# Batch 0's first token product by halves of 256 channels, second-product blocks in banks of their own

## The chip, the cores and the metric

The kernel runs on one core of a Trainium2 chip. The metric is the device time of one execution in microseconds; a comparison takes the median of several. The engines are named as in the profile: PE (matmul), PEld (its weight loads), DVE, ACT, POOL, and SP, the engine that issues nearly all DMAs here.

## The reference

Attention over 8 batches, 8 heads, 576 positions and 64 channels a head, then an MLP mixer. Heads 0 to 3 see the last 32 positions (local), heads 4 to 7 see every 32nd position (strided).

```
x   = softmax(mask(q k^T / 8)) v         # x: 576 x 512 per batch, local heads give channels 0-255
h   = relu(x^T w_tok1) w_tok2            # tokens 576 -> 256 -> 576
u   = x + h^T
out = u + relu(u w_ch1) w_ch2            # channels 512 -> 1536 -> 512
```

The four weight matrices come as float64 and are converted on the chip.

## The kernel before

**Products.** Each fp32 factor is split into a high part and the rest (`h` and `l`, type fp32r), and a product is three matmuls: high by high, rest by high, high by rest.

**Names.** `w1` and `w2` are the channel weights `w_ch1` and `w_ch2`, `t1` and `t2` the token weights. `tok1` is the first token product for a batch: it splits x in five chunks of 128 positions (`split`, L555: a high copy on ACT, L559, and a subtraction on DVE, L565), multiplies by t1 (L577), and ends with a relu on ACT and its rest on DVE (L585, L586). `tok2` is the second token product of one block `cc` of 128 channels: it transposes x's block into a PSUM bank (L611), adds six matmuls with t2 (L616), and `split_u` (L594 on ACT, L595 on DVE) splits the sum into `uh` and `ul`. `mlp` runs 12 up-projections (`up_proj`, L815, w1 by columns of 128, relu at L818, rest at L819) and 12 down-projections (`down_proj`, L827, w2), alternating.

**Weights.** `convert` takes one piece of 512 numbers per partition: a DMA (L118), two ACT operations (L128, L131), one DVE operation (L129), and then the join: one DVE operation (L133), an ACT cast to the high part (L142, for the short last piece of t1 L157) and a POOL subtraction for the rest (L143). A generator yields between these three parts. A piece of w1 here is 256 columns of two of the four channel chunks, so up-projections 0 and 1 need two pieces together. There are five pieces of t1 and t2, and 24 of w1 and w2, beside a small tail of t2.

**The opening.** Batch 0's attention, the t1, t2 and first w1 conversions and batch 0's token products stand in one written-out order of generator steps (`steps(...)`, L747 to L769). The order of emission is the order on each engine, SP's queue of DMAs included. `s0`, `s1` are the strided head pairs (`strided_pe`), `l0`, `l1` the local ones (`local_first`); `e` are the weight pieces of the opening, `pieces` those that follow inside batch 0's MLP, two of them begun at each step of `do_pieces`; `mix` is `tok1`, `mixes` (called m0 to m3 in the prediction) are the four `tok2` blocks. The strided result goes to DRAM (L441) and is loaded back (`load_x`, L545, L548); the local result is written into x in SBUF directly (L311), but the last 64 positions go through small DMAs (L309), because `tok1` wants them twice, on partitions 0 to 63 and 64 to 127. `keep_busy` issues idle matmuls (L710).

`tok1` covers all 512 channels in one go. The `tok2` blocks take their PSUM from `Halves`, which deals the two banks of one tile to two blocks:

```
t = pair()
self.left += [t[:, 0], t[:, 1]]
```

The last step of `tok2` for a block issues its six matmuls and its split together:

```
us.append(split_u(pool, pu, apart if turned else []))
yield
```

Batches 1 to 7 do the same products inside the MLP of the batch before (`do_tok1`, `do_tok2`); the strided heads of batches 2 to 7 run on POOL and DVE beside it.

Of the kernel before, what the change touches and what calls it, by code (L numbers as in the profile page):

```python
# [10 lines left out]
F32 = mybir.dt.float32  # L11
# [10 lines left out]
HL = 4  # L22
# [11 lines left out]
WARM = 10  # L34
# [24 lines left out]
def attn_mixer_kernel(ctx, tc, qkT, vw, qkU, vU, qs, ks, vs, qksT, vsP, mask, mask2, w1, w2, wt1, wt2, outT):  # L59
# [111 lines left out]
    def w1_piece(raws, q, c):  # L171

        fs = slice(2 * P * q, 2 * P * q + 2 * P)
        return load_split(raws, lambda: (w1h[:, c:c + 2, fs], w1l[:, c:c + 2, fs]), DM, chunks(w1, c, fs))
# [86 lines left out]
    def local_first(pool, pairs, p, hp, into, masks):  # L261
# [44 lines left out]
        nc.vector.tensor_tensor(out=x_t, in0=av[:, :, n - 1, :D], in1=mz[:, :, n - 1:].to_broadcast([P, 2, D]), op=ALU.mult)  # L306
        x = x_t.rearrange("p j d -> p (j d)")
# [78 lines left out]
    def strided_pe(pool, banks, b, hp, loaded, s_t):  # L386
# [45 lines left out]
        for l in range(2):  # L432
            nc.vector.tensor_tensor(
                out=x_t[:, l::2], in0=sums[l][:, :, :D].rearrange("p (c j) d -> p c j d", j=2),
                in1=mz[:, l].rearrange("p (c j) -> p c j", j=2).unsqueeze(3).to_broadcast([P, NBP // 2, 2, D]), op=ALU.mult)
        x = x_t.rearrange("p m j d -> p m (j d)")
# [105 lines left out]
    def load_x(x_t, b, cs):  # L542
# [4 lines left out]
        for r in range(2):  # L547
            nc.sync.dma_start(out=x_t[64 * r:64 * r + 64, NSC - 1, cs], in_=src[P * (NSC - 1):])  # L548

    def tok1(pool, ps_t, x_t, h, cs, lead=2, room=None):  # L550
# [4 lines left out]
        def split(c):  # L555
            x = x_t[:, c, cs]
            xhl = (room(c) if room else pool.tile([P, 2, DM], F32, name="xhl")).bitcast(F32R)
            xh = xhl[:, 0, :n]
            nc.scalar.copy(out=xh, in_=x)  # L559
            if c == NSC - 1:  # L560
# [3 lines left out]
            xlo = xhl[:, 1, :n]  # L564
            apart.append(nc.vector.tensor_tensor(out=xlo, in0=x, in1=xh.bitcast(F32), op=ALU.subtract))  # L565
            return ((t1h, xh), (t1l, xh), (t1h, xlo))

        ahead = [split(0)]
        yield
        ahead += [split(c) for c in range(1, lead)]  # L570
        ph = [ps_t.tile([P, 512], F32, name="t")[:, :n] for _ in range(2)]
        for c in range(NSC):

            terms = ahead.pop(0)
            for k, (l, r) in enumerate(terms):
                for m in range(2):
                    nc.tensor.matmul(  # L577
                        ph[m], l[:, c, P * m:P * m + P], r, start=(c == 0 and k == 0), stop=(c == NSC - 1 and k == 1))
# [26 lines left out]
    def tok2(pool, ps_t, x_t, h, cc, us, turned):  # L605
# [60 lines left out]
    pieces = [t2_tail, *(lambda raws, c=c: w2_piece(raws, c) for c in range(2))]  # L666
    for k in range(2, 6):
        pieces += [lambda raws, k=k, c=c: w1_piece(raws, k, c) for c in (0, 2)]
        pieces += [lambda raws, c=c: w2_piece(raws, c) for c in (2 * k - 2, 2 * k - 1)]
    pieces += [lambda raws, c=c: w2_piece(raws, c) for c in range(10, NFC)]  # L670
# [14 lines left out]
    with tc.tile_pool(name="first", bufs=2) as first, \  # L685
         tc.tile_pool(name="raws", bufs=4, side="right") as raws, \
# [6 lines left out]
        nc.sync.dma_start(out=mask2_sb, in_=mask2)  # L693
        loaded = [strided_load(first, 0, hp) for hp in range(2)]
        nc.sync.dma_start(out=mask_sb, in_=mask)
# [3 lines left out]
        nc.gpsimd.tensor_copy(  # L699
            out=mask2_b[:, :RP * (NBP - 1)].rearrange("p (c k) -> p c k", k=RP), in_=mask2_sb[:, :RP].unsqueeze(1).to_broadcast([P, NBP - 1, RP]))  # L700
        nc.gpsimd.tensor_copy(out=mask2_b[:, RP * (NBP - 1):], in_=mask2_sb[:, RP:])
        for c in range(NSC):
            nc.gpsimd.tensor_copy(out=masks[:, 64 * c:64 * c + 64], in_=mask_sb[:, FIRST.get(c, 0)])

# [3 lines left out]
        def keep_busy(n):  # L708
            for _ in range(n):
                nc.tensor.matmul(idle_t, still[:, :P], still, start=True, stop=True)  # L710

        class Halves:

            left = []

            def tile(self, shape, dtype, name):
                if not self.left:
                    t = pair()
                    self.left += [t[:, 0], t[:, 1]]
                return self.left.pop(0)  # L720
# [8 lines left out]
        keep_busy(WARM)  # L729
# [3 lines left out]
        s0, s1 = (strided_pe(first, banks, 0, hp, loaded[hp], e_ts[hp]) for hp in range(2))  # L733
        l0, l1 = (local_first(first, ps_p, 0, hp, x_t, masks) for hp in range(2))
        e = [t1_piece(raws, 0), t1_piece(raws, 2), t1_short(raws), t2_piece(raws, 0), t2_piece(raws, 1)]
        e += [w1_piece(raws, q, c) for q in range(2) for c in (0, 2)]

        def room(c):
            return xp.tile([P, 2, DM], F32, name="xhl") if c < 2 else first.tile([P, 2, S], F32, name="eqk") if c < 4 else first.tile([P, 1, 4 * NSC * DV], F32, name="lv")

        mix = tok1(xp, ps_m, x_t, h, slice(0, DM), lead=3, room=room)

        def steps(*gens):
            for g in gens:
                next(g, None)

        steps(l0, l1, l0, l1, *e[:4])  # L747
        steps(s0)
        keep_busy(1)
        steps(s1)  # L750
        keep_busy(1)
# [356 lines left out]
```

## Time and profile before

| | |
|---|---|
| median of 3 runs | 808.65 us (807.28 to 808.75) |
| the profiled execution's own time | 808.64 us |
| its span in the profile | 806.8 us |
| PE busy | 772.2 us (96%) |
| DVE, ACT, POOL busy | 460.5, 240.6, 379.8 us |
| mean granted TensorE clock | 0.989 of full speed |
| chain that ended last | PE 73%, DVE 9%, DMA 5%, POOL 4%, ACT 4%, issue 3% |

A busy share is an average over stages. Times below are us from the span's start unless marked ns. "idle before <-X" names what ended the idle time of an engine; "issue" is idle time for which the profile shows no releaser. [...]

### The profile page before, as it was taken

To read this page: it belongs to the slowest core of one execution; us is meant where nothing else is said; L and a number is where in the kernel's file an instruction comes from. 1 tells how busy PE (TensorE), PEld (TensorE's weight loads), DVE (VectorE), ACT (ScalarE), POOL (GpSimd) and SP (SyncE) were. 2 spreads that over 40 slices of the span, in tenths; PEclk is the share of its full clock that TensorE was granted. 3 is DMA by queue.
4 is the path that set the end of the run, shared out by engine and by line. 5 is a ranking of instruction groups with operands and counts; after the bars stand their busy time and mean duration, and the time that the engine had idled before them with its cause. 6 is when DMAs were issued, how large, how long until landed. Compare 5 with 4: busy or idle time off the path is not lost.

```text
span 806.8 us, 14535 instructions
## 1 busy us (share of the span) xinstructions
PE 772.2 (96%) x5887; PEld 622.0 (77%) x5892; DVE 460.5 (57%) x954; ACT 240.6 (30%) x489; POOL 379.8 (47%) x287
## 2 busy tenths in 40 slices
PE   7659999999999999999999999999999999999998
PEld 4537777777778888888788888788888888888886
DVE  4544666777598677786678667776652234113112
ACT  3556775232122312232223122332123222112110
POOL 1223355959785884678558946776600000202000
PEclk9979999999999999999999999999999999999999
DMA  9456855234822282248305520755042212101001
GB/s 322 143 189 223 252 172 202 82 138 124 246 67 95 67 241 78 70 125 260 122 24 173 174 82 1 226 161 158 1 125 76 82 46 72 53 1 52 1 1 52
DMA packets 70059, 96.40 MB, mean 119 GB/s; under 512 B 33640, under 2 KB 41960, under 8 KB 69992
## 3 DMA queue, kind: packets, MB, share of 16 engines
q1 hardware_dynamic: 69416, 93.57, 37.2%
q10 hardware_dynamic: 576, 1.90, 0.6%
q8 instruction: 46, 0.75, 0.4%
q14 instruction: 21, 0.17, 0.1%
HBM read 67.86 MB, written 27.46 MB: 118 GB/s over the span
## 4 chain that ended last, share of the span: by engine, by line
PE 73%; DVE 9%; DMA 5%; POOL 4%; ACT 4%; issue 3%; SPq 1%; ACTq 0%; DVEq 0%; POOLq 0%
PE acc L827 29%; PE h L815 27%; PE t L616 4%; POOL sprod L452 4%; PE t L577 4%; PE t L815 2%; DMA x<-x 2%; DVE w_f L133 1%; DVE sa L532 1%; PE t L358 1%; ACT w_rest L128 1%; DVE xhl L565 1%; PE t L334 1%; DMA sa<-in_vs 1%; DVE ss L505 1%
## 5 line engine op out<-in xcount | busy, mean ns | idle before, releaser
L452 POOL TENSOR_TENSOR sprod<-sa,ss 128x576 f32<-128x576 f32 (+8 forms) x108 | 153.4, 1466 | 84.7 <-issue 48.7
L452 POOL TENSOR_TENSOR sprod<-sa 128x576 f32<-128x576 f32 (+8 forms) x108 | 160.5, 1518 | 36.9 <-DVE ss L505 11.5
L827 PE MATMUL acc<-gh,w2h 128*128 128x512 f32 x432 | 170.5, 395 | 0.0
L819 DVE SCALAR_TENSOR_TENSOR gl<-h,gh 128x512 fp32r<-128x512 f32 x99 | 68.0, 687 | 179.3 <-ACT gh L818 179.1
L827 PE MATMUL acc<-gh,w2l 128*128 128x512 f32 x432 | 168.4, 390 | 0.0
L827 PE MATMUL acc<-gl,w2h 128*128 128x512 f32 x432 | 168.3, 390 | 0.0
L815 PE MATMUL h<-uh,w1h 128*128 128x512 f32 x396 | 158.5, 400 | 4.1 <-DVE gl L819 2.7
L815 PE MATMUL h<-ul,w1h 128*128 128x512 f32 x396 | 154.9, 391 | 0.0
L815 PE MATMUL h<-uh,w1l 128*128 128x512 f32 x396 | 154.9, 391 | 0.0
L818 ACT ACTIVATE gh<-h 128x512 fp32r<-128x512 f32 x99 | 59.1, 597 | 292.5 <-PE h L815 292.5
L505 DVE TENSOR_REDUCE ss<-sprod 128x9 f32<-128x576 f32 (+8 forms) x108 | 80.4, 777 | 27.8 <-POOL sprod L452 27.6
L827 PEld LDWEIGHTS acc<-gh,w2l 128*128 128x128 f32 x432 | 81.1, 188 | 17.1
L827 PEld LDWEIGHTS acc<-gh,w2h 128*128 128x128 f32 x432 | 81.1, 188 | 17.1
L827 PEld LDWEIGHTS acc<-gl,w2h 128*128 128x128 f32 x432 | 81.2, 188 | 16.5 <-DVE gl L819 0.2
L815 PEld LDWEIGHTS h<-uh,w1h 128*128 128x128 f32 x396 | 74.7, 189 | 23.1 <-DVE gl L819 4.8
L532 DVE TENSOR_REDUCE sa<-sprod 128x64 f32<-128x576 f32 (+8 forms) x108 | 80.2, 776 | 17.5 <-POOL sprod L452 17.1
L815 PEld LDWEIGHTS h<-ul,w1h 128*128 128x128 f32 x396 | 74.7, 189 | 16.1
L815 PEld LDWEIGHTS h<-uh,w1l 128*128 128x128 f32 x396 | 74.8, 189 | 14.7
L644 POOL TENSOR_TENSOR x<-x,xhl 128x512 f32<-128x512 f32 x4 | 5.0, 1280 | 116.1 <-DMA x<-u 116.1
L577 PE MATMUL t<-xhl,t1h 128*128 128x512 f32 x134 | 42.2, 398 | 6.8 <-ACT xhl L559 3.1
L565 DVE TENSOR_TENSOR xhl<-x,xhl 128x512 fp32r<-128x512 f32 x30 | 29.9, 1014 | 11.3 <-ACT xhl L559 11.3
L577 PEld LDWEIGHTS t<-xhl,t1h 128*128 128x128 f32 x134 | 24.3, 188 | 15.3 <-ACT xhl L559 5.3
(177 smaller groups left out, 859.2 us busy)
## 6 DMA issues: line engine op xcount, KB each, us to landing
out_t<-ot SPq DMA_DIRECT2D x35, 256.0 KB
w_raw<-in_w SPq DMA_DIRECT2D x17, 512.0 KB
lqk<-in_qkU SPq DMA_DIRECT2D x9, 832.0 KB
x<-x SPq DMA_DIRECT2D x28, 256.0 KB
lv<-in_vU SPq DMA_DIRECT2D x9, 780.0 KB
xhl<-in_w SPq DMA_DIRECT2D x7, 512.0 KB
x<-lv SPq DMA_DIRECT2D x36, 96.0 KB
xtl<-lv SPq DMA_DIRECT2D x36, 96.0 KB
```

Of the source, the lines that this page charges most:

```text
L128: nc.scalar.activation(out=y_b[:, :, 0], in_=raw_b[:, :n, 3], func=AF.Identity, bias=below, scale=1.0 / 32)
L133: nc.vector.scalar_tensor_tensor(out=a, in0=a, scalar=3, in1=y, op0=ALU.logical_shift_left, op1=ALU.bitwise_xor)
L452: i = nc.gpsimd.tensor_tensor(op=op, **operands)
L505: nc.vector.tensor_reduce(out=s_t[:, i, :i + 1], in_=pr.rearrange("p (n d) -> p n d", d=D), axis=AX.X, op=ALU.add)
L532: nc.vector.tensor_reduce(out=o_t[:, i], in_=pr.rearrange("p (d n) -> p d n", n=i + 1), axis=AX.X, op=ALU.add)
L565: apart.append(nc.vector.tensor_tensor(out=xlo, in0=x, in1=xh.bitcast(F32), op=ALU.subtract))
L577: nc.tensor.matmul(ph[m], l[:, c, P * m:P * m + P], r, start=(c == 0 and k == 0), stop=(c == NSC - 1 and k == 1))
L616: nc.tensor.matmul(pu, l[:, cs], r[:, m, :MAIN], start=(turned and m == 0 and k == 0), stop=(m == 1 and k == 2), skip_group_check=True)
L815: nc.tensor.matmul(ph, l[:, cc, fs], r, start=(cc == 0 and k == 0), stop=(cc == NCC - 1 and k == 2))
L818: nc.scalar.activation(out=gh, in_=ph, func=AF.Relu)
L819: nc.vector.scalar_tensor_tensor(out=gl, in0=ph, scalar=0.0, in1=gh.bitcast(F32), op0=ALU.max, op1=ALU.subtract)
L827: nc.tensor.matmul(acc[cc], l[:, fc, cs], r, start=(fc == 0 and k == 0), stop=(fc == NFC - 1 and k == 2))
```

## The change

- `tok1` for batch 0 runs twice, over 256 channels each: `L` for the local half, `S` for the strided half. All five splits of a half are issued ahead of its matmuls. The last 64 positions are taken once, on partitions 0 to 63, with three terms; the copies to partitions 64 to 127 are gone.
- Each `tok2` block takes a tile of two banks for itself and uses its first bank. Its split is a generator step of its own, after its matmuls.
- A w1 piece is 128 columns of all four channel chunks, the weights of one up-projection. Three are begun in the opening ahead of the last splits, where there were four of the old shape; the `pieces` of the MLP alternate w1 and w2.
- Loads, stores, conversions, attention steps and idle matmuls stand in a new order, one token a generator step; `e0` to `e2` are t1, `e3` and `e4` t2, `e5` to `e7` w1, `p0` to `p3` the first of `pieces`, `x` the reload of the strided half, `b` an idle matmul. 8 idle matmuls at the start, not 10; 6 raw buffers, not 4.

```
-WARM = 10
+WARM = 8
...
+    def w1_piece(raws, fc):
+        fs = slice(P * fc, P * fc + P)
+        return load_split(raws, lambda: (w1h[:, :, fs], w1l[:, :, fs]), DM, w1[:, fs].bitcast(U32).rearrange("(c p) n -> p c n", p=P))
...
-        for r in range(2):
-            nc.sync.dma_start(out=into[64 * r:64 * r + 64, NSC - 1, cs], in_=x[:64])
-        nc.sync.dma_start(out=xd[0][S:S + 64, cs], in_=x[64:])
         nc.vector.tensor_tensor(
             out=into[:, :n - 1, cs].rearrange("p c (j d) -> p j c d", d=D), in0=av[:, :, :n - 1, :D],
             in1=mz[:, :, :n - 1].unsqueeze(3).to_broadcast([P, 2, n - 1, D]), op=ALU.mult)
+        for ps, to in ((slice(0, 64), into[:64, n - 1, cs].rearrange("p (j d) -> p j d", d=D)), (slice(64, P), x_t[64:])):
+            nc.vector.tensor_tensor(out=to, in0=av[ps, :, n - 1, :D], in1=mz[ps, :, n - 1:].to_broadcast([64, 2, D]), op=ALU.mult)
+        yield
+        nc.sync.dma_start(out=xd[0][S:S + 64, cs], in_=x_t[64:].rearrange("p j d -> p (j d)"))
...
+            rows = slice(0, 64 if room and c == NSC - 1 else P)
+            x = x_t[rows, c, cs]
...
-            if c == NSC - 1:
+            if c == NSC - 1 and not room:
...
+            return ((t1h[rows], xh), (t1l[rows], xh), (t1h[rows], xlo))
...
-        ahead = [split(0)]
+        ahead = [split(c) for c in range(1 if lead < NSC else NSC)]
         yield
-        ahead += [split(c) for c in range(1, lead)]
+        ahead += [split(c) for c in range(len(ahead), lead)]
...
             nc.vector.tensor_tensor(out=x_t[:, cc], in0=pu, in1=x_t[:, cc], op=ALU.add)
-            yield
             pu = x_t[:, cc]
-        us.append(split_u(pool, pu, apart if turned else []))
+        yield
+        us[cc] = split_u(pool, pu, apart if turned else [])
         yield
...
-    pieces = [t2_tail, *(lambda raws, c=c: w2_piece(raws, c) for c in range(2))]
...
+    pieces = [lambda raws: w1_piece(raws, 3), lambda raws: w2_piece(raws, 0), t2_tail, lambda raws: w2_piece(raws, 1)]
+    for k in range(4, NFC):
+        pieces += [lambda raws, k=k: w1_piece(raws, k), lambda raws, c=k - 2: w2_piece(raws, c)]
...
+        class Half:
+            def tile(self, shape, dtype, name):
+                return pair()[:, 0]
...
+        gens["L"] = tok1_half(slice(0, HL * D), "eqk", "eqk", "ev", "ev", "es")
+        gens["S"] = tok1_half(slice(HL * D, DM), "xhl", "xhl", "lqk", "lqk", "es")
+        for cc in range(NCC):
+            gens[f"m{cc}"] = tok2(up0, Half(), x_t, h, cc, u, False)
...
+        order = """
+            s0 s1 s1 l0 s0 s0 s1 e0 s0 l0 e0 l0 s0 l1 e1 s1 b e2 l0 e0 e1 l1 l1 b s1 e3 e2 e4 l1 b b e1 s0 s1 e2 e3 e5
+            l0 l1 e4 b b b b m0 L x L L L e3 L e4 L l0 m1 S m3 m0 e6 m0 S e5 S S S e7 e6 S m2 e5 m1 m2 e6 p0 m3 m1 l1 m2 m3 e7 e7
+            p1 p2 p3 p0"""
+        for i, k in enumerate(order.split()):
+            if i == 3:
+                masks_in()
+            next(gens[k], None)
```

## Rows read from the trace of the kernel before

**Rows 1.** Busy time by stage: us, then engines, clock, DMA share, GB/s.
```profile
30.40:60.90 30.50, 19.55 (x73) 13.33 (x73) 14.55 (x29) 17.92 (x32) 8.71 (x8) 0.83 0.53 184
60.90:120.00 59.10, 56.74 (x645) 43.44 (x646) 35.70 (x113) 43.19 (x84) 22.87 (x19) 0.97 0.69 215
120.00:806.00 686.00, 674.99 (x4623) 551.12 (x4621) 395.74 (x786) 168.59 (x358) 343.41 (x243) 1.00 0.34 103
```

**Rows 2.** PE's timeline in the opening: start, us, instructions, idle before.
```profile
15.57 0.81 PE L276 MATMUL pair<-lqk 64*32 64x64 f32 x58 [1.20 <-issue]
...
23.18 1.16 PE L422 MATMUL pair<-ev,es 64*64 64x65 f32 x33 [4.52 <-issue]
...
30.59 1.07 PE L611 MATMUL pair<-ident,x 128*128 128x128 f32 x8 [0.94 <-DVE x L311]
...
39.17 1.07 PE L577 MATMUL t<-eqk,t1h 128*128 128x512 f32 x4
...
44.39 0.39 PE L616 MATMUL pair<-t2h,hl 128*128 128x512 f32 x1
48.90 0.79 PE L616 MATMUL pair<-t2h,hh 128*128 128x512 f32 x1 [4.12 <-DVE ul L595]
...
56.95 0.50 PE L616 MATMUL pair<-t2h,hh 128*128 128x512 f32 x1 [2.67 <-DVE ul L595]
...
60.89 0.79 PE L815 MATMUL h<-uh,w1h 128*128 128x512 f32 x1 [1.40 <-DVE ul L595]
```

**Rows 3.** DVE's timeline: the last write of x's local channels.
```profile
29.77 0.68 DVE L311 TENSOR_TENSOR x<-pair,lm 128x512 f32<-128x512 f32 x1
```

**Rows 4.** DMA queues from 13 to 14.3 us: packets, MB, share.
```profile
q1 hardware_dynamic: 114, 0.51, 97.6%
q8 instruction: 1, 0.02, 5.2%
```

**Rows 5.** DMA queues from 20.3 to 22 us.
```profile
q8 instruction: 1, 0.02, 3.9%
```

**Rows 6.** Busy time by stage: a stretch with a full DMA queue.
```profile
39.00:49.00 10.00, 5.21 (x21) 3.19 (x19) 4.80 (x8) 6.46 (x12) 3.40 (x3) 0.91 1.04 392
```

**Rows 7.** SyncE's queue: x's strided half stored and loaded again.
```profile
19.52 8.65 SPq L441 DMA_DIRECT2D x<-ex  x12
...
29.61 2.05 SPq L545 DMA_DIRECT2D x<-x  x4
```

**Rows 8.** ACT's timeline ahead of the first block's split.
```profile
46.27 0.87 ACT L128 ACTIVATE w_rest<-w_raw,small 128x512 uint8<-128x512 uint8 x1
...
47.55 0.56 ACT L594 CAST uh<-pair 128x512 fp32r<-128x512 f32 x1
```

**Rows 9.** Busy time by stage: the two later stretches at the lower clock.
```profile
47.20:54.10 6.90, 5.20 (x12) 3.80 (x12) 2.31 (x4) 1.80 (x4) 0.52 (x1) 0.51 0.42 162
...
57.40:64.30 6.90, 5.50 (x14) 3.80 (x13) 1.89 (x5) 3.63 (x7) 2.58 (x2) 0.51 0.55 166
```

**Rows 10.** Groups by line, first 61 us: busy us, mean ns, idle before.
```profile
L128 ACT ACTIVATE w_rest<-w_raw,small 128x512 uint8<-128x512 uint8 x8 | 7.0, 875 | 0.6 <-DMA w_raw<-in_wt 0.6
L133 DVE SCALAR_TENSOR_TENSOR w_f<-w_f,w_rest 128x512 uint32<-128x512 uint32 x8 | 5.5, 687 | 0.7 <-ACT w_f L131 0.5
L131 ACT ACTIVATE w_f<-w_raw 128x512 f32<-128x512 f32 x8 | 5.1, 642 | 0.0
...
L595 DVE TENSOR_TENSOR ul<-pair,uh 128x512 fp32r<-128x512 f32 x4 | 2.8, 692 | 10.0 <-ACT uh L594 10.0
...
L143 POOL TENSOR_TENSOR t2l<-w_f,t2h 128x512 fp32r<-128x512 f32 x2 | 2.6, 1288 | 6.3 <-ACT t2h L142 6.3
...
L565 DVE TENSOR_TENSOR xhl<-x,xhl 128x512 fp32r<-128x512 f32 x2 | 1.5, 813 | 2.1 <-ACT xhl L559 2.1
...
L565 DVE TENSOR_TENSOR eqk<-x,eqk 128x512 fp32r<-128x512 f32 x2 | 1.3, 676 | 0.0
...
L157 ACT CAST t1h<-w_f 128x256 fp32r<-128x256 f32 x1 | 0.4, 402 | 0.0
```

More of the change, by code (lines that the diff above doesn't have):

```diff
@@ L384, in strided_load, with strided_pe @@
         return qk_t[:, 0], qk_t[:, 1], v_t
-    def strided_pe(pool, banks, b, hp, loaded, s_t):
+    def strided_pe(pool, banks, b, hp, loaded, s_t, split=False):
         q_t, k_t, v_t = loaded
@@ L545, in load_x @@
             nc.sync.dma_start(out=x_t[:, c, cs], in_=src[P * c:P * c + P])
-        for r in range(2):
+        for r in range(copies):
             nc.sync.dma_start(out=x_t[64 * r:64 * r + 64, NSC - 1, cs], in_=src[P * (NSC - 1):])
@@ L577, in tok1 @@
                     nc.tensor.matmul(
-                        ph[m], l[:, c, P * m:P * m + P], r, start=(c == 0 and k == 0), stop=(c == NSC - 1 and k == 1))
+                        ph[m], l[:, c, P * m:P * m + P], r, start=(c == 0 and k == 0), stop=(c == NSC - 1 and k == len(terms) - 1))
             if c + lead < NSC:
@@ L698, in attn_mixer_kernel, with keep_busy @@
         nc.vector.memset(e_ts[1], 0.0)
[L699 to L703, printed above, removed]
-        idle_t = ps_m.tile([P, 512], F32, name="t")
[L708 to L720, printed above, removed]
+        nc.sync.dma_start(out=mask2_sb, in_=mask2)
+        idle_t = ps_m.tile([P, 512], F32, name="t")
+        def keep_busy():
+            nc.tensor.matmul(idle_t, still[:, :P], still, start=True, stop=True)
         def pair():
@@ L727, in banks @@
             return [t[:, 0], t[:, 1]], [(slice(0, 2), t)]
-        keep_busy(WARM)
+        class Half:
+            def tile(self, shape, dtype, name):
+                return pair()[:, 0]
+        for _ in range(WARM):
+            keep_busy()
         x_t = xp.tile([P, NSC, DM], F32, name="x", bufs=1)
         h = new_h(xp)
-        s0, s1 = (strided_pe(first, banks, 0, hp, loaded[hp], e_ts[hp]) for hp in range(2))
-        l0, l1 = (local_first(first, ps_p, 0, hp, x_t, masks) for hp in range(2))
@@ L735, in attn_mixer_kernel @@
[L735 to L745, printed above, removed]
@@ L766, in attn_mixer_kernel, with strided_first @@
-        steps(e[3], e[7], mixes[0], mixes[1], mix)
-        keep_busy(4)
-        steps(mix, e[3], e[4], e[8], mix, mixes[2], mixes[3], e[4], mix, mix, mix, e[5], e[5], e[6], *pieces[:4])
-        steps(mixes[0], mixes[1], e[6], e[7], mixes[2], e[7], e[8], mixes[3], pieces[0], e[8])
+        u = [None] * NCC
+        def strided_first(hp):
+            qk_t = first.tile([P, 2, S], F32, name="eqk")
+            nc.sync.dma_start(out=qk_t, in_=qksT[0, hp])
+            yield
+            v_t = first.tile([P, NBP // 2, 2, 2, DV], F32, name="ev")
+            nc.sync.dma_start(out=v_t, in_=vsP[0, hp])
+            yield
+            yield from strided_pe(first, banks, 0, hp, (qk_t[:, 0], qk_t[:, 1], v_t), e_ts[hp], split=True)
@@ new lines, in room, with tok1_half, reload, busy @@
+        def room(names):
+            shapes = dict(eqk=[P, 2, S], ev=[P, 2, NSC * DV + DV], es=[P, 2, 32 * NBP * 2], lqk=[P, 2, NSC * P + 32], xhl=[P, 2, DM])
+            return lambda c: (xp if names[c] == "xhl" else first).tile(shapes[names[c]], F32, name=names[c])
+        def tok1_half(cs, *names):
+            return tok1(xp, ps_m, x_t, h, cs, lead=NSC, room=room(names))
+        def reload():
+            load_x(x_t, 0, slice(HL * D, DM), 1)
+            yield
+        def busy():
+            while True:
+                keep_busy()
+                yield
@@ new lines, in attn_mixer_kernel @@
+        gens = dict(x=reload(), b=busy())
+        for hp in range(2):
+            gens[f"s{hp}"] = strided_first(hp)
+            gens[f"l{hp}"] = local_first(first, ps_p, 0, hp, x_t, masks)
+        for i, g in enumerate([t1_piece(raws, 0), t1_piece(raws, 2), t1_short(raws), t2_piece(raws, 0), t2_piece(raws, 1)]):
+            gens[f"e{i}"] = g
+        for fc in range(3):
+            gens[f"e{5 + fc}"] = w1_piece(raws, fc)
+        for i in range(4):
+            gens[f"p{i}"] = pieces[i]
```

53 lines of the change are left out of this document (15 added, 38 removed).

## The prediction, on record before the result

> **What bounds the kernel now.** I read the table by stages first, then PE's timeline in the opening, then what ACT, DVE, POOL and SyncE did in PE's gaps. From 60.9 us on PE is busy 56.7 of 59.1 us, and then 675.0 of 686 [rows 1]: the MLP blocks run on PE almost without a hole, and an edit there must shorten PE's own work. Up to 60.9 nothing is that full: between 30.4 and 60.9 PE is busy 19.6 of 30.5 us, ACT 17.9, DVE 14.6, DMA share 0.53 [rows 1]. That is a chain through several engines, ending when the first w1 product starts at 60.89 [rows 2]. Everything behind hangs on that moment, so the question is when it comes; what it gains the span gains, if the MLP of batch 0 doesn't give it back.
>
> I cut the opening in two at 30.4, when DVE has written the second half of x's local channels [rows 3].
>
> **Up to 30.4: no gain taken.** PE stands still 1.20 us before 15.57 and 4.52 us before 23.18 with no engine or data named ("issue") [rows 2]. Some 1.5 us before PE goes on, at both, a 16 KB packet has passed on the instruction queue [rows 4, 5]; I infer that PE waited for its own program. The second stall, in the second strided product, is what brings x to 30.4. The new order reaches the same product with nearly the same number of instructions before it, so I expect the same stall there, though its first loads are put differently (a t1 piece ahead of the second local pair's keys, both t2 pieces ahead of x's stores). The two missing warm-up matmuls, the earlier start of the strided scores and the earlier l0 transposes all end before that stall and are worth nothing. l1's keys come later by one 0.5 MB piece, about 1.3 us at the 392 GB/s of a full queue [rows 6], and that ends in the stall too. The stores of x's strided half hang on the stalled product as before: issued from 19.52 on, the reload from 29.61 [rows 7]. In front of the reload there is now one w1 piece, again about 1.3 us; x lands near 34, and is wanted near 35. Hidden, with about 1 us of cover; past that, one for one, because the transposes of m3, which stand ahead of m0's product on PE, wait for it.
>
> [...]
>
> **From 30.4 to 60.9: what is removed.** [...]
> - Before, the first token product waits for both halves of x, and its splits stand on ACT behind the t1 and t2 conversions. Now the local half needs no DMA at all.
> - The second-product blocks share a pair of banks, and one block's split is issued together with its products. So m1's first matmul waited 4.12 us and m3's 2.67 us for the split of the block before [rows 2], and that split stood on ACT behind a w1 conversion: the 0.87 us row and its partner run until 47.55, though m0's last product had started at 44.39 [rows 2, 8]. With a bank for each, and the split a step later, m1, m2 and m3 run on: 6.8 us of waits go.
> [...]
>
> **What is added.** 60 matmuls of 256 columns instead of 28 of 512 (three terms for the last 64 rows, no longer two). The trace has no 256-column matmul of this kind. The 512-column ones follow each other every 0.227 us ((1.07 - 0.39)/3, the 0.39 being one matmul's own length) [rows 2]. Bounds: half of that, 0.114, and all of it. I take 0.12, near the lower end, because transposes of 128 columns, which load weights of 128 x 128 each time too, take at most 0.134 (1.07/8, the last one's tail counted in) [rows 2]. [...]
>
> **The new chain, in us of the span,** with durations from [rows 10] and PE at its full clock:
> 1. From 30.2 the five splits of the local half: ACT 0.40 each (the 256-column row), DVE about 0.4, between half and the whole of its 0.68 for 512 columns. PE has its first pair near 30.7, and 30 x 0.12 = 3.6, held up a little by DVE: 34.5.
> 2. Relu and its rest, 0.4 + 0.4 and a hand-over: 35.4. m0's six products wait for t2's second low half. That is the last of a chain behind DVE's splits: two joins of 0.69, a cast, POOL 1.28 twice, to 36.4. m0 ends at 37.1.
> 3. The strided half's splits ran meanwhile; its 30 matmuls: 40.7.
> 4. Its relu and rest lie beside m2's transposes and m1's six products (0.5 + 6 x 0.227 = 1.9): 42.6. m2 and m3, 12 x 0.227 = 2.7: 45.3.
> 5. The last split, ACT 0.56 [rows 8] + DVE 0.69 + 0.2 of hand-over: 46.8.
> 6. Handing over and contention: of two pairs of like subtractions one has a mean of 813 ns and one 676 [rows 10]; I add 0.7 for some ten such steps. The first up-projection starts at **47.5**.
>
> Against 60.9 that is 13.4. PE is dense from 37 to 45, so I take the full clock for the first up-projection: 3.4 us at half speed before [rows 9] are worth 1.7 more.
>
> **What is given back.** Three w1 pieces of 128 columns are begun ahead of the last splits where four pieces were; the third's conversion and half of the fourth's now stand on ACT behind the last split and ahead of the first relu: 2 x (0.88 + 0.64) + 0.6 = 3.6 by their rows [rows 10], with 2.7 us of up-projection over it. The relu is late by about 1, and the same later for DVE and the joins. ACT is busy 43.2 of 59.1 us in that stage [rows 1], so it recovers. Cost: 0 to 3.6; I take 1.0, as PE has two up-projections to go before it needs the first relu. The w1 pieces are as many bytes and conversions as before, with rows of 1 KB where they had 2 KB; DMA has room (0.69 share [rows 1]). Later pieces keep leads of 2.5 to 5 blocks of twelve matmuls. Nothing else in batches 1 to 7 changes its order on any engine: the additional yield in the second product only moves a split's issue, and splits follow one another as before.
>
> Sum: 13.4 + 1.7 - 1.0 = 14.1. The profiled execution took 808.64 us (span 806.8), within 0.01 of the median; 808.64 - 14.1 = **794.5 us**.
>
> **Rivals.**
> - *No stall, or a shorter one:* the second local half then waits for its loads and ACT's conversions, so at most about 4 of the 4.5 us come back: 790.5. For it: the new order changes what DMA carries at that moment. Against: the stall's place in the program stays.
> - *256 columns cost what 512 do:* 60 x (0.227 - 0.12) = 6.4 more: 801. For it: each still loads a full block of weights, and no row shows that 256 columns hide it. Against: the transposes' pace.
> - *Batch 0's MLP gives back some of it:* fewer pieces ahead; if relus and joins stay late by the 3.6 us, and up-projections 2 and 3 wait for w1 in turn, some 6 are lost: 800.5. Against: ACT's 16 us of idle time in that stage.
> - *Slower:* instruction blocks wait behind data. If each further block that PE needs comes only when the data queue is empty, the stall grows, for the opening's loads now follow one another with fewer holes. It decides when PE's stalls together exceed today's 5.7 by more than 14.1 us; waiting for the last opening loads, near 45, would put the up-projection near 63 and the time at 810. Against: the first packet [rows 4] went through while the data queue was at 97.6%.
>
> **Chances.** Forecast 0.62 (own range 791 to 799: the bounds of 256 columns below, of the give-back, and a stretch at 1.2 GHz, worth 1.7 to 3.4); shorter stall 0.10; dear 256 columns 0.10; given back 0.11; slower 0.07. The range 790 to 803 leaves out the slower case and the tails of the first and the third. Measurements of this kernel tell changes of about 0.2% (1.6 us): faster 0.91, within it 0.03, slower 0.06.
>
> **What would show it.** Right: the first w1 product near 47.5 at the full clock, second products of the four blocks with no wait for another block's split, a 256-column matmul every 0.12 us, the 4.5 us issue stall still there. Wrong: a longer or missing stall; a matmul pitch near 0.23; PE gaps before up-projections 2 and 3; m3's transposes waiting for the reload.

## The result, and the profile of the changed kernel

798.26 us (median of four runs, 797.42 to 799.21) against 808.1 us: ratio 0.988, interval 0.9862 to 0.9896, so 9.8 us faster. Forecast were 794.5 us, a gain of 14.1. The profiled execution, the longest of the four (799.21), has a span of 797.4 us, 9.4 less than before, and that is the difference the rows below account for.

Busy time by stage of the kernel after; the columns are those of [rows 1]:

```profile
30.40:44.20 13.80, 13.80 (x92) 12.21 (x91) 9.30 (x21) 9.49 (x20) 4.55 (x4) 1.00 0.87 281
44.20:120.00 75.80, 70.71 (x700) 53.94 (x699) 44.26 (x127) 53.65 (x102) 29.63 (x24) 0.95 0.71 223
120.00:797.50 677.50, 663.85 (x4569) 542.51 (x4568) 391.46 (x778) 162.18 (x347) 338.13 (x239) 1.00 0.32 99
```

The stretch from 30.4 to the first w1 product is 13.8 us long, where [rows 1] show 30.5, and PE fills all of it. But PE is idle for 5.1 us of the next 75.8 and for 13.7 us behind that; before it was 2.4 us in the MLP's first 59 and 11 behind [rows 1].

PE's timeline of the opening after, against [rows 2]:

```profile
20.70 0.69 PE L421 MATMUL pair<-ev,es 64*64 64x65 f32 x29 [1.48 <-issue]
...
29.15 0.50 PE L579 MATMUL t<-eqk,t1h 128*128 128x256 f32 x2 [0.90 <-ACT eqk L561]
...
30.03 0.74 PE L579 MATMUL t<-eqk,t1h 128*128 128x256 f32 x4
...
40.09 0.47 PE L618 MATMUL pair<-t2h,hh 128*128 128x512 f32 x1
...
44.30 0.39 PE L825 MATMUL h<-uh,w1h 128*128 128x512 f32 x1
```

The stall in the second strided product is 1.48 us where it was 4.52. The local half's product runs from 29.15, the blocks m1 to m3 from 40.09 without a wait, and the first up-projection starts at 44.30, with nothing idle before it. The split of the last block, on DVE, ends behind that start, at 45.8:

```profile
45.12 0.69 DVE L597 TENSOR_TENSOR ul<-pair,uh 128x512 fp32r<-128x512 f32 x1 [0.61 <-ACT uh L596]
```

To find where the rest went I laid PE's order of work side by side at the same products. First come four landmarks of the kernel before (a fifth stands in [rows 2]), then those of the kernel after:

```profile
69.90 0.50 PE L815 MATMUL h<-uh,w1h 128*128 128x512 f32 x1
...
80.52 0.50 PE L815 MATMUL h<-uh,w1h 128*128 128x512 f32 x1
...
146.72 0.60 PE L611 MATMUL t<-ident,x 128*128 128x128 f32 x4
...
150.73 0.39 PE L827 MATMUL acc<-gh,w2h 128*128 128x512 f32 x1
```

```profile
51.62 0.50 PE L825 MATMUL h<-uh,w1h 128*128 128x512 f32 x1
...
66.43 0.50 PE L825 MATMUL h<-uh,w1h 128*128 128x512 f32 x1
...
132.76 0.60 PE L613 MATMUL t<-ident,x 128*128 128x128 f32 x4
136.81 0.66 PE L613 MATMUL t<-ident,x 128*128 128x128 f32 x4 [3.45 <-DVE hl L588]
...
141.65 0.40 PE L837 MATMUL acc<-gh,w2h 128*128 128x512 f32 x1
```

| landmark on PE | before | after | lead |
|---|---|---|---|
| first up-projection [rows 2] | 60.89 | 44.30 | 16.6 |
| third up-projection | 69.90 | 51.62 | 18.3 |
| fourth up-projection | 80.52 | 66.43 | 14.1 |
| batch 1's second token product | 146.72 | 132.76 | 14.0 |
| first down product behind it | 150.73 | 141.65 | 9.1 |
| end of the span | 806.8 | 797.4 | 9.4 |

So the opening and the first two up-projections gave 18.3 us, more than forecast, and 4.2 and 4.9 us were given back in two places. From 141.65 to the end the lead changes by 0.3 us only.

**First place, 50 to 62 us.** PE's waits there, and ACT's timeline:

```profile
54.15 0.30 PE L197 MATMUL t<-lqk 64*32 64x64 f32 x2 [0.87 <-DVE gl L829]
55.24 0.45 PE L197 MATMUL t<-lqk 64*32 64x64 f32 x30 [0.80 <-DVE es L401]
...
58.91 0.80 PE L632 MATMUL t<-hh,t2h 128*128 128x512 f32 x1 [0.75 <-POOL t2h L143]
```

```profile
48.96 0.58 ACT L828 ACTIVATE gh<-h 128x512 fp32r<-128x512 f32 x1
...
52.28 0.60 ACT L142 CAST w2h<-w_f 128x512 fp32r<-128x512 f32 x1
52.79 0.58 ACT L828 ACTIVATE gh<-t 128x512 fp32r<-128x512 f32 x1
56.12 0.76 ACT L404 ACTIVATE es<-es 128x648 f32<-128x648 f32 x1 [2.75 <-DVE es L401]
```

The second up-projection's last product ends at 49.9, and its relu comes at 52.79: between the two relus ACT has two conversions and two casts of weight pieces. Its rest on DVE comes late, then DVE's reductions of the strided scores, then the exponential (ACT idle 2.75 us), then t2's tail, and PE waits 0.87, 0.80 and 0.75 us. In the same piece of work the kernel before has one wait of this size:

```profile
77.89 0.44 PE L224 MATMUL t<-ident,ls 128*128 128x128 f32 x2 [1.03 <-ACT es L413]
```

That makes 1.4 us more of waiting. The rest of the 4.2 us, 2.8, is clock (an estimate: the 5.65 us in which PE is busy at 0.51 would be 2.9 at 1.00):

```profile
56.00:62.40 6.40, 5.65 (x17) 4.15 (x16) 2.60 (x14) 4.80 (x12) 0.46 (x1) 0.51 0.66 218
```

After the first two of these gaps PE was granted 0.51 of its clock for 6.4 us; the third gap lies inside that stretch. (A stretch at 0.51 is what the prediction's chances and relu_first's expectation call one at 1.2 GHz; the profiles show the share alone, no frequency.)

**Second place, 130 to 141 us.** ACT's, DVE's and POOL's timelines of the kernel after:

```profile
132.37 0.62 ACT L142 CAST w2h<-w_f 128x512 fp32r<-128x512 f32 x1 [3.10 <-DVE w_f L133]
134.91 0.62 ACT L142 CAST w2h<-w_f 128x512 fp32r<-128x512 f32 x1 [1.92 <-DVE w_f L133]
135.44 1.08 ACT L587 ACTIVATE hh<-t 128x512 fp32r<-128x512 f32 x2
...
130.31 2.03 DVE L133 SCALAR_TENSOR_TENSOR w_f<-w_f,w_rest 128x512 uint32<-128x512 uint32 x1
...
133.59 1.30 DVE L133 SCALAR_TENSOR_TENSOR w_f<-w_f,w_rest 128x512 uint32<-128x512 uint32 x1
136.06 1.29 DVE L588 SCALAR_TENSOR_TENSOR hl<-t,hh 128x512 fp32r<-128x512 f32 x2 [1.18 <-ACT hh L587]
...
128.31 3.48 POOL L453 TENSOR_TENSOR sprod<-sa 128x512 f32<-128x512 f32 x2
```

The relu of batch 1's token product stands on ACT behind the casts of the last two weight pieces, each of which waits for its join on DVE. Before, one such cast stood there, the relu followed at 145.12, and PE waited 0.18 us:

```profile
144.59 0.62 ACT L142 CAST w2h<-w_f 128x512 fp32r<-128x512 f32 x1 [2.67 <-DVE w_f L133]
...
147.50 0.66 PE L611 MATMUL t<-ident,x 128*128 128x128 f32 x4 [0.18 <-DVE hl L586]
```

The changed opening begins one w1 piece fewer, so the list that batch 0's MLP works off has 22 pieces in place of 21, and the 22nd's join falls at step 18.5, ahead of that relu. PE waits 3.45 us, and its 12 second products behind that take 4.4 us where they took 2.8, partly at the lower clock (0.50 from 138.0 to 141.4): 3.3 more of waiting and 1.6 of clock are the 4.9. The two joins took 2.03 and 1.30 us beside POOL's instructions, for 0.69 with none of POOL's beside them [rows 10]; how much of the wait is owed to that, and not to their place, no run takes apart.

### The profile page after: what moved, and what is told of

Read it like the earlier page. It is cut to its first block, busy times and chain, and to the rows that moved or that the text cites. A ratio compares the mean times of both kernels' runs of the same rounds, so it can differ in the third digit from the quotient of the medians.

```text
span 797.4 us, 14592 instructions
## 1 busy us (share of the span) xinstructions
PE 770.7 (97%) x5916; PEld 623.6 (78%) x5916; DVE 463.4 (58%) x963; ACT 241.4 (30%) x496; POOL 379.4 (48%) x287
## 4 chain that ended last, share of the span: by engine, by line
PE 76%; DVE 9%; DMA 5%; POOL 4%; issue 2%; ACT 2%; SPq 1%; DVEq 0%; ACTq 0%; POOLq 0%
PE acc L837 31%; PE h L825 28%; PE t L618 5%; PE t L579 5%; POOL sprod L453 4%; PE t L825 2%; DMA w_raw<-in_wt 2%; DMA sa<-in_qs 1%; PE t L357 1%; DVE sa L533 1%; DVE xhl L567 1%; PE t L632 1%; DVE w_f L133 1%; DVE w_rest L129 1%; DVE ss L506 1%
## 5 line engine op out<-in xcount | busy, mean ns | idle before, releaser
L837 PEld LDWEIGHTS acc<-gh,w2l 128*128 128x128 f32 x432 | 81.2, 188 | 17.2
L533 DVE TENSOR_REDUCE sa<-sprod 128x64 f32<-128x576 f32 (+8 forms) x108 | 80.1, 777 | 17.2 <-POOL sprod L453 16.9
L579 PE MATMUL t<-xhl,t1h 128*128 128x512 f32 (+1 forms) x134 | 41.2, 390 | 5.1 <-DVE xhl L564 2.5
L561 ACT CAST xhl<-x 128x512 fp32r<-128x512 f32 (+1 forms) x37 | 21.9, 609 | 42.7 <-PE t L579 36.4
L567 DVE TENSOR_TENSOR xhl<-x,xhl 128x512 fp32r<-128x512 f32 (+1 forms) x30 | 29.3, 996 | 9.2 <-ACT xhl L561 9.2
```

Of the source, the lines that this page charges most:

```text
L533: nc.vector.tensor_reduce(out=o_t[:, i], in_=pr.rearrange("p (d n) -> p d n", n=i + 1), axis=AX.X, op=ALU.add)
L579: nc.tensor.matmul(ph[m], l[:, c, P * m:P * m + P], r, start=(c == 0 and k == 0), stop=(c == NSC - 1 and k == len(terms) - 1))
L837: nc.tensor.matmul(acc[cc], l[:, fc, cs], r, start=(fc == 0 and k == 0), stop=(fc == NFC - 1 and k == 2))
```

## The experiments

All ratios are to the kernel before, run beside on the same chip; the change itself has 0.9879.

**The two losses.** Two kernels put the last pieces elsewhere, one puts the second relu first, one does two of these.

tail_early:

```
-            at(int(1.8 * i) / 2, do_pieces, i)
+            at(int(1.8 * i) / 2 - (0, 0.5, 0.5, 1)[max(0, i - 18)], do_pieces, i)
```

> The last three weight pieces go half a block, half a block and one block of twelve matmuls earlier (16.5, 17.5, 17.5 in place of 17, 18, 18.5). Theory: the 3.45 us in which TensorE waits for batch 1's second token product, near 133, comes from the casts of the last two pieces, which stand on ScalarE ahead of the token product's relu; moved ahead they leave it, the gap falls below 1 us and the stretch at the lower clock behind it goes: 798.3 - 4 = about 794 us. Rival 1: VectorE is full there with its reductions and joins, and what comes earlier is only paid earlier: the gap stays over 2.5 us, time within 1.6 us of 798.3. Rival 2: the gap belongs to the GpSimd products that share time with VectorE, same outcome.

802.04 us, 0.9926 (0.9899 to 0.9953): slower than the change. PE's timeline:

```profile
133.60 1.22 PE L579 MATMUL t<-xhl,t1h 128*128 128x512 f32 x2 [7.20 <-DVE xhl L564]
```

The gap didn't shrink, it moved to the token product itself and doubled. The joins, 3.68 us for two on DVE at 126.96, and their casts on ACT, the second at 130.68, now stand ahead of the split of x's last rows (ACT 131.69, DVE 132.54). The first rival had DVE full, and it is busy 8.79 of 10 us from 120 to 130; but what comes earlier is not only paid earlier, it hurts an earlier consumer, and more.

tail_late:

```
-            at(int(1.8 * i) / 2, do_pieces, i)
+            at({20: 19, 21: 19.5}.get(i, int(1.8 * i) / 2), do_pieces, i)
```

> The last two weight pieces are joined later, at steps 19 and 19.5 in place of 18 and 18.5, so that both stand behind batch 1's token-product relu. Theory of ScalarE's order: the relu no longer waits for two casts, TensorE's 3.45 us gap near 133 falls to under 1 us, 794 us or a little less. Rival: VectorE is the one that is late, whatever order; then the gap only shrinks by the one join taken from in front of it (1.3 us) and the time stays at 796.5 to 798.

796.38 us, 0.9847 (0.9831 to 0.9862). The wait ahead of L613 is gone altogether, and the clock from 130 to 140 is 1.00. In this profile the lead at the first down product behind is 15.9 us, in place of 9.1. Then PE waits anew:

```profile
154.74 1.16 PE L333 MATMUL t<-lqk 64*32 64x64 f32 x94 [1.35 <-DVE x L634]
162.42 0.50 PE L825 MATMUL h<-uh,w1h 128*128 128x512 f32 x1 [0.82 <-DVE gl L829]
```

So the order on ACT and DVE was the cause of the gap, as the theory said, though the time lies nearer to the rival's 796.5 than to its 794: 2.2 us of waiting come back where DVE, behind with its strided sums (busy 9.96 of 10 us from 150 to 160), comes late to the next consumer. The same kernel has the code of the change up to 120 us, with the three waits of the first place (0.87, 0.80 and 1.61 us), but a clock of 1.00 there:

```profile
56.00:62.00 6.00, 4.39 (x21) 3.35 (x22) 3.09 (x15) 5.22 (x13) 0.45 (x1) 1.00 0.88 269
```

Its lead falls by 2.3 us in the first place, not by 4.2: 1.9 us of the change's first loss is a stretch at a granted 0.51 that the same code doesn't always get. (By itself the stretch costs the 2.8 us estimated above, but the third wait is shorter beside it, 0.75 us for 1.61.)

relu_first:

```
-            at(int(1.8 * i) / 2, do_pieces, i)
+            at(1 if i < 2 else int(1.8 * i) / 2, do_pieces, i)
```

> In batch 0's MLP the conversion of the second, third and the join of the first two weight pieces go behind the second relu (steps 1 and 1 in place of 0 and 0.5). Theory: ScalarE's backlog put the second relu 2.9 us behind the end of its products, from which TensorE's gaps near 53 to 59 (0.87, 0.80, 0.75 us) and then the stretch at 1.2 GHz from 56.4 to 62.4 came; with the relu first the gaps and the stretch go, the lead over the kernel before stays near 18 up to the first down-projection, and the time falls by 3.5 to 4.5 us, to 794 or 794.5. Rival: the conversions are needed as early as this; put off by one block, the t2 tail or the first w2 piece comes late and TensorE waits there instead: within 1.6 us of 798.3.

797.14 us, 0.9856 (0.9839 to 0.9873), not to be told from the change by time alone. ACT and PE:

```profile
48.98 0.60 ACT L828 ACTIVATE gh<-t 128x512 fp32r<-128x512 f32 x1 [0.39 <-PE t L825]
...
53.25 0.45 PE L197 MATMUL t<-lqk 64*32 64x64 f32 x30 [0.71 <-DVE es L401]
56.85 0.50 PE L632 MATMUL t<-hh,t2h 128*128 128x512 f32 x1 [1.56 <-POOL t2h L143]
```

The relu now follows its products, the 0.87 wait is gone, 0.80 became 0.71, and the clock stays at 1.00. The tail product's wait stays: t2's tail is converted no earlier. Against the 3.28 us of waits in tail_late's profile 2.27 remain, so the backlog was worth 1.0 us in waits; the theory named the right relu but put too much on it. Its profile has a clock of 0.66 from 130 to 140, the change's 0.90, which takes away some of that win.

both (relu_first and tail_early together):

> Both edits, the relu ahead of the conversions at the start of batch 0's MLP and the last three pieces earlier at its end. If both theories hold the two gains add: 798.3 - 8 = about 790 us. If the second loss only takes up what the first gives back (the pieces all run ahead of a fixed limit of VectorE's), about 794.

799.7 us, 0.9888 (0.9863 to 0.9914). Neither number came. The waits of 0.71 and 1.56 us are those of relu_first, the 7.20 us wait at L579 that of tail_early; the two places don't act on each other.

combined (relu_first, tail_late, and batch 0's tail product from step 2 to 3):

```
-        at(2 if b == 0 else 0, tok2_tail, ps_t, x_t, h, b)
+        at(3 if b == 0 else 0, tok2_tail, ps_t, x_t, h, b)
...
-                at(int(1.8 * i) / 2, do_pieces, i)
+                at({0: 1, 1: 1, 20: 19, 21: 19.5}.get(i, int(1.8 * i) / 2), do_pieces, i)
```

> The second relu of batch 0's MLP ahead of the conversions, the tail product of batch 0 one block later (step 3 in place of 2), and the last two weight pieces behind batch 1's token-product relu. If the losses are independent: relu_first won some 1.1 us in TensorE's waits, the tail product's wait of 1.56 goes as well, and tail_late won 4.9 less the 2.15 that VectorE's strided sums gave back near 153 and 161: 798.3 - 1.1 - 1.5 - 2.7 = 793 us, ratio to the kernel before 0.981. Rival: the strided sums on VectorE are a limit of their own in 115 to 165, and whatever is won ahead of it is waited for near 153: the lead at batch 1's tenth block stays at 13.9 us as in tail_late, 796 us, ratio 0.985.

793.3 us, 0.9819 (0.9801 to 0.9838), a clear gain over the change. In the first place the 0.71 us wait is left, beside a new one of 0.34 at 61.84; the lead at the fourth up-projection is 17.8 us, and at the first down product behind batch 1's token product 18.3. The limit near 150 holds as in tail_late, at the same two places:

```profile
152.28 1.15 PE L333 MATMUL t<-lqk 64*32 64x64 f32 x94 [1.36 <-DVE x L634]
159.96 0.50 PE L825 MATMUL h<-uh,w1h 128*128 128x512 f32 x1 [0.86 <-DVE gl L829]
```

But it takes 2.1 us of the lead and not everything that was won ahead of it: in tail_late the lead there was 15.9 us ahead of the two waits and 13.8 behind them, here 18.3 and 16.3. The rival, a fixed limit, falls.

strided_earlier (combined, and `if b or i >= 14` in place of 16 ahead of some_strided):

> The combined kernel with the strided lane of batch 2 begun two blocks earlier (steps from 14 in place of 16). The combined kernel lost 2.1 us of its lead near 151 and 159, where TensorE waits for VectorE. Theory: the strided sums are late there because they begin late; begun earlier the two waits (1.36 and 0.86) shrink below 0.4 each and the time falls to 791.5 or so, ratio 0.9795. Rival: earlier sums take VectorE from the last weight pieces and the token product's splits, and the waits come back between 108 and 130: 793 us or more.

797.5 us, 0.9853 (0.9826 to 0.988): the rival. The first wait near 150 (now at 162) falls to 0.62 us and the second is gone, but two waits ahead of them grow, from 1.15 to 1.87 us at 110 and from 1.07 to 2.36 at 133, and two are new, 2.52 us at 120 and 2.71 at 140:

```profile
139.87 0.66 PE L613 MATMUL t<-ident,x 128*128 128x128 f32 x4 [2.71 <-DVE hl L588]
```

**The parts of the change.**

shared_banks:

```
-            def tile(self, shape, dtype, name):
-                return pair()[:, 0]
+            def tile(self, shape, dtype, name):
+                if not self.left:
+                    t = pair()
+                    self.left += [t[:, 0], t[:, 1]]
+                return self.left.pop(0)
...
+        half = Half()
...
-            gens[f"m{cc}"] = tok2(up0, Half(), x_t, h, cc, u, False)
+            gens[f"m{cc}"] = tok2(up0, half, x_t, h, cc, u, False)
```

> Only the banks are undone: the second-product blocks share a pair of banks again, two by two, in the new order with the split a step later. If it is the shared bank that made TensorE wait (4.12 and 2.67 us in the kernel before, as the prediction put it), waits of that kind come back ahead of the blocks behind the first, up to 6.8 us, and the time goes to 803 to 805. Rival: the order does it, since now no product has a split of the same pair still open ahead of it: no such wait over 0.3 us, time within 1.6 us of 798.3.

798.07 us, 0.9875 (0.9854 to 0.9897). ACT, then PE:

```profile
44.88 0.59 ACT L596 CAST uh<-pair 128x512 fp32r<-128x512 f32 x1 [1.31 <-PE pair L618]
...
47.68 0.47 PE L831 MATMUL h<-uh,w1h 128*128 128x512 f32 x1 [2.84 <-DVE ul L597]
```

No second product waits: of the 6.8 us none comes back there. Instead the third block's split waits until the products of the fourth, in the same pair, are done, and the up-projection until the last split is done. The banks are thus worth 2.8 us at this place. The time didn't show it: the waits of 0.87 and 0.80 us in the first place are gone, since ACT catches up while PE waits, so 1.5 us are left at the fourth up-projection (lead 14.2, against 15.7 in tail_late), and in the profile its clock was 0.998 on the mean, the change's 0.991.

shared_split_now (the same, and each split right behind its products):

```
- ... m0 e6 m0 S e5 S S S e7 e6 S m2 e5 m1 m2 e6 p0 m3 m1 l1 m2 m3 e7 e7
+ ... m0 m0 e6 S e5 S S S e7 e6 S m2 e5 m1 m1 m2 m2 e6 p0 m3 m3 l1 e7 e7
```

> The banks shared as above, and each block's split issued right behind its products, as in the kernel before. If bank and order act together: m3's first product waits for m2's split, about 1.5 us (ScalarE 0.56, VectorE 0.69, handing over 0.2), the others for nothing since m0's split is done long before; time 799.5 to 800.5. If the banks alone: 6.8 us as above. If neither: within 1.6 us of 798.3, and the waits of the kernel before came from the conversions ahead of the splits alone.

800.16 us, 0.9902 (0.9884 to 0.992), as the first case had it:

```profile
44.11 0.50 PE L618 MATMUL pair<-t2h,hh 128*128 128x512 f32 x1 [1.40 <-DVE ul L597]
47.27 0.47 PE L831 MATMUL h<-uh,w1h 128*128 128x512 f32 x1 [1.49 <-DVE ul L597]
```

A wait of one split, 1.4 us, is what the shared bank cost this product, with nothing else ahead of the split; the second line, 1.49 us, is the up-projection waiting for the last split. By the rows of before, the rest of the 4.12 and 2.67 us [rows 2] was what stood on ACT ahead of the split: m0's last product ended at 44.78 [rows 2], its split began at 47.55 [rows 8], 2.8 us later. The order takes that away; this part is worked out from the rows and not run by itself.

whole (batch 0's first token product in one go of 512 columns, 28 products, ahead of all second products):

```
-        gens["L"] = tok1_half(slice(0, HL * D), "eqk", "eqk", "ev", "ev", "es")
-        gens["S"] = tok1_half(slice(HL * D, DM), "xhl", "xhl", "lqk", "lqk", "es")
+        gens["S"] = tok1_half(slice(0, DM), "xhl", "xhl", "eqk", "eqk", "lv")
...
-            l0 l1 e4 b b b b m0 L x L L L e3 L e4 L l0 m1 S m3 m0 e6 m0 S e5 S S S e7 e6 S m2 e5 m1 m2 e6 p0 m3 m1 l1 m2 m3 e7 e7
+            l0 l1 e4 b b b b m0 x e3 e4 l0 m1 S m3 e6 S e5 S S S S m0 e7 m0 e6 m2 e5 m1 m2 e6 p0 m3 m1 l1 m2 m3 e7 e7
```

> Batch 0's first token product in one go of 512 columns, begun when the strided half of x is back, with everything else of the change left in. By the prediction's terms the local half's 30 products of 256 columns (29.2 to 33.6 in the profile) then lie behind the reload: with the 28 products of 0.227 (6.4 us) in place of 3.9 for the second half, and m0 behind them, the first up-projection comes 2.5 to 4 us later, 47 to 48, time 801 to 802.5. Rival: the halves are hidden anyway, ScalarE's and VectorE's conversions of t2 and w1 set the time of the up-projection: it stays near 44.5, time within 1.6 us of 798.3.

804.06 us, 0.9954 (0.9936 to 0.9972), 5.8 us above the change, more than either number expected.

```profile
31.52 1.59 PE L613 MATMUL pair<-ident,x 128*128 128x128 f32 x4 [2.23 <-DMA x<-x]
...
49.42 0.39 PE L824 MATMUL h<-uh,w1h 128*128 128x512 f32 x1
```

The up-projection comes 5.1 us later. PE waits 2.23 us for the reload and then has the 28 products ahead of it, the first of them at a granted clock of 0.66 on the mean from 30 to 35; later m2's transposes wait 1.40 us for m0's split, which frees their bank. By this run the halves are the larger part of the change, 5.8 of its 9.8 us, with these two counted in: they fill the time of the reload. The parts need not add up.

w1_square (the old cut of the w1 pieces, 256 columns of two row blocks):

```
-        return load_split(raws, lambda: (w1h[:, :, fs], w1l[:, :, fs]), DM, w1[:, fs]. ...)
+        return load_split(raws, lambda: (w1h[:, c:c + 2, fs], w1l[:, c:c + 2, fs]), DM, chunks(w1, c, fs))
```

> Only the cut of the w1 pieces is undone: 256 columns of two row blocks each as in the kernel before, so that an up-projection needs two pieces where it needed one; the same number of pieces, begun in the same places. Theory: the cut by 128 columns is worth nothing here. GpSimd has the first two pieces' low halves at 43.4 and 44.7, the first up-projection's second half wants the second one at 45.7 and nothing waits; the first up-projection comes near 44.5 and the time is within 1.6 us of 798.3 (ratio 0.986 to 0.990). Rival: it is what lets the products begin; then TensorE waits for GpSimd's low halves inside the first or third up-projection, 1 to 3 us, ratio 0.990 to 0.992.

797.21 us, 0.9849 (0.9822 to 0.9877): the cut is worth nothing here. The wait at batch 1's second product is there as in the change, 3.46 us, and the list still has 22 pieces. PE's timeline, then the stage from 130 to 140:

```profile
135.29 0.66 PE L613 MATMUL t<-ident,x 128*128 128x128 f32 x4 [3.46 <-DVE hl L588]
...
130.00:140.00 10.00, 6.54 (x34) 5.31 (x33) 7.92 (x12) 3.89 (x7) 8.72 (x8) 1.00 0.42 133
```

But the clock stays at 1.00 here, and the 12 second products behind the wait take 2.8 us, as in the kernel before. Like the 1.9 us in the first place, the 1.6 us of clock in the second don't come with every such wait: this profile has the change's waits in both places at full clock, and gives back 5.9 us (a lead of 18.2 at the third up-projection, 12.3 at the end) where the change's gives back 8.9.

**The stall named "issue".** In the profiles of the eleven kernels that have the change's order up to there it stands ahead of the same product, 29 from the end of L421's second run, and is between 0.59 and 3.33 us; the two 16 KB packets of the instruction queue ahead of it (46 packets, 0.75 MB in the whole execution, before and after; that they carry PE's program is inferred from the stalls) pass 6.9 to 7.6 us apart (10.70 and 18.07 in the change, 13.01 and 20.59 before), and the third follows 3.8 to 6.0 us behind. Two kernels alter what the data queue carries, and leave PE's order; light_queue also puts the t1 conversions later.

light_queue:

```
- ... s0 l1 e1 s1 b e2 l0 e0 e1 l1 l1 b s1 e3 e2 e4 l1 b b e1 s0 s1 e2 e3 e5
+ ... s0 l1 s1 b l0 e0 l1 l1 b s1 l1 b b s0 e1 e2 e3 e4 s1 e1 e2 e1 e2 e3 e5
```

> The loads of four weight pieces (two t1, two t2, 1.6 MB) go behind the first strided stores, so that the data queue runs empty near 15 in place of 24. In the traces so far the second 16 KB instruction packet comes 7.0 to 7.6 us after the first and TensorE stands still before the 29th-last product of L421 for 0.6 to 4.5 us. Theory A: the packet waits behind the data; then it comes 2 to 5 us after the first, and the stall at that product is gone (under 0.3 us). Theory B: TensorE's program has a pace of its own, some 7.3 us for 16 KB whatever the queue carries: the packets stay 7.0 to 7.6 us apart and the stall at that product is 1 us or more. The kernel itself should be slower by 2 to 6 us, since the t1 conversions come late.

800.35 us (one run). PE, and the queues from 15.9 to 17.2 us:

```profile
17.92 1.23 PE L421 MATMUL pair<-ev,es 64*64 64x65 f32 x48 [0.25 <-ACT t1h L142]
...
26.21 1.31 PE L298 MATMUL pair<-lv,ls 64*32 64x65 f32 x70 [3.70 <-issue]
```

```profile
q1 hardware_dynamic: 116, 0.29, 56.7%
q8 instruction: 1, 0.02, 4.9%
```

All 48 products run in one go; the packet passed at 16.09, 4.5 us after the first, just as the data queue, full until then (share 1.05 from 14 to 16), had thinned out. The next one, with the moved loads now in the queue, passed 7.2 us later, and the stall appears at the next boundary, 3.70 us.

heavy_queue:

```
- ... l1 l1 b s1 e3 e2 e4 l1 b b e1 s0 s1 e2 e3 e5
+ ... l1 l1 b s1 e3 e2 e4 e5 e6 l1 b b e1 s0 s1 e2 e3
...
- ... m3 m0 e6 m0 S e5 S S S e7 ...
+ ... m3 m0 m0 S e5 S S S e7 ...
```

> Two more pieces (1 MB of w1) are loaded ahead of the strided stores, so that the queue stays full some 2.6 us longer. Theory A: the third instruction packet, 3.8 to 6.0 us after the second so far, comes 6 us or more after it, and TensorE stands still by issue ahead of L298 or the first local products. Theory B: it comes 3.8 to 6 us after it as before. The strided half comes back up to 2.6 us later; the first up-projection moves by 0 to 2 us.

799.17 us (one run). The third packet passed 6.5 us after the second (17.84, 24.36), and PE stood still:

```profile
26.83 0.93 PE L298 MATMUL pair<-lv,ls 64*32 64x65 f32 x70 [2.06 <-issue]
```

Both go with the first theory, light_queue clearly, heavy_queue narrowly: 6.5 us against up to 6.0, and a wait of 2.06 us at a product where the change's own order shows up to 1.51. A fixed pace of some 7.3 us is out. That data in the queue is what holds a packet back is likely and not shown: in light_queue the share of the data queue was 1.02 over the 4.5 us between the first two packets and 0.76 over the 7.2 us behind them, and when PE asks for a packet no profile tells. Why the stall differs between 0.59 and 3.33 us with one and the same order these runs don't settle.

## Why the prediction was right in kind and 4 us off

- **Up to 30.4, "no gain".** Wrong, in two steps: that the same place in the program means the same stall, and that the stall is what brings x. The stall was 1.48 us for 4.52; as the same order has 0.59 to 3.33 in eleven profiles, its size here is in part luck. x's local half was complete at 28.85 (DVE, 28.58 + 0.27) in place of 30.45 [rows 3], but a shorter stall didn't bring it: in those profiles it was complete between 27.90 and 29.69, at 28.61 with the stall of 3.33 (tail_early), at 29.69 with one of 0.75 (both). Other waits take its place, in the change those for l0's and l1's exponentials (1.61 and 1.01 us). Which part of the new order makes x earlier stays open. In light_queue one packet passed without a stall, at 16.09, and all 48 products ran on; elsewhere the stall at this place was 0.59 to 4.52 us.
- **256 columns at 0.12 us.** Right: four in 0.74 us, (0.74 - 0.40) / 3 = 0.113; over the second half, with the steps between its tiles, 30 from 35.84 to 39.68, 0.128.
- **The chain of five steps.** Durations right within 0.6 us. L ended near 33.5, m0 35.8, S 39.7, m1 41.6, m3 44.3; the forecast was 34.5, 37.1, 40.7, 42.6, 45.3, later by 1.0 to 1.3 throughout, where x was forecast 1.6 later than it came. The reload stayed hidden, as forecast: m3's transposes ran at 33.50 with m1's, without a wait.
- **"The last split, 46.8", and 0.7 of handing over: 47.5.** Wrong by 2.2 us. The step put the last split ahead of the up-projection. The up-projection started behind m3's last product; the fourth block is read only by its last three products, from 46.34, when the split was done (45.8). shared_banks shows the forecast's case: with the split on the path PE waits 2.84 us and starts at 47.68.
- **Shared banks, 6.8 us.** The waits went, but the term's owner was wrong: shared_split_now prices the bank alone at one split, 1.4 us a time. The order took the rest.
- **The clock, 1.7.** Right: the lead grew from 16.6 to 18.3 over the first two up-projections. (Before, the last four of m3's products ran at the lower clock too and are not in this term.) That a dense PE is granted the full clock, on which the term rests, no run shows: PE had 1.00 while busy for all of 30.4 to 44.2, but 0.50 while busy for all of 28 to 30 in light_queue.
- **Given back, 1.0.** This is the term that failed: 8.9, or 5.9 where the clock stayed full (w1_square). Half was at the place it named. It reckoned with one late relu and with ACT's idle time over the stage; the first was late by 1.8 (its products ended at 47.2), the second by 2.9, and an average of idle time doesn't help an instruction that stands behind conversions. The other half lies under "nothing else in batches 1 to 7 changes its order": I counted bytes and conversions, which are equal, but not the pieces left for the MLP, 22 for 21, nor where the last one falls.

In sum 16.6 + 1.7 - 8.9 = 9.4, where the forecast had 13.4 + 1.7 - 1.0 = 14.1. Two errors work against each other here, 3.2 us too little for the opening and 7.9 too little given back, and that the time came within 4 us is in part luck. The rival of a shorter stall had its condition come true, but not its 4 us: x came 1.6 earlier, and 1.0 of that was left at the end of m3's products. The rival "batch 0's MLP gives back some of it" was right in kind (800.5), through the late relu it named and, near the end of the same MLP, through a second place that it didn't; the waits for w1 that it expected didn't come. The rival of dear 256 columns fell. That of instruction packets behind data pointed the right way in light_queue and heavy_queue, but its condition, that each packet waits until the queue is empty, doesn't hold: the change's own came at 18.07 while the queue was full (share 1.01 from 17.8 to 19.3). The stall didn't grow, so the slower case didn't come.

Open: why the stretches from 56 to 62 us and behind the wait at 136.81 were granted 0.51 and 0.50 in the change's profile, and 1.00 in others with the same waits (tail_late, w1_square).

## What to carry to other kernels

Work moved out of a tuned opening has to be followed to the step where it now falls: list the deferred items, count them, and see which engine has them ahead of something due. The wait of 4.12 us at a shared bank was, by the rows of before, 2.8 us of what stood ahead of the split on ACT and the split itself; in shared_split_now, with the banks still shared and a new order, only the split's own length was left, 1.4 us. Deferring a piece past the instruction that is due (tail_late) helped, hurrying it (tail_early) hurt an earlier one: beside a DVE busy 8.8 of 10 us, look at who comes next.

## What the runs showed of the hardware

- The instruction queue passed packets of 16 KB, 46 with 0.75 MB in all, before and after. PE went on from its two stalls 2.5 to 2.6 us after the start of a packet (13.01 and 20.59, then 15.57 and 23.18 before; 10.70 and 18.07, then 13.20 and 20.70 after); that the packets were its program is inferred from this. From stall to stall 126 matmuls with their weight loads passed before, 127 after. In this order the first two packets ahead of the stall were 6.9 to 7.6 us apart and the third 3.8 to 6.0 behind; with loads moved away from that stretch (light_queue, one run) they were 4.5 apart and the third 7.2 behind.
- The join on DVE, 0.69 us with no POOL instruction beside it [rows 10], took 2.03 us beside POOL's products (128.31 to 131.79) and 1.30 beside a subtraction of POOL's (133.07 to 134.34), ending 0.55 us behind each. Why it is longer there these rows don't show.
- The same code ran from 56 to 62 us at a granted clock of 0.51 in one profile and of 1.00 in another (the change, tail_late). Behind a wait of 3.4 to 3.5 us the same second products had 0.66 on the mean from 130 to 140 in one profile and 1.00 in another (relu_first, w1_square).
